# Sixteen dummy matmuls ahead of the first transposes in a fused attention and MLP kernel

## The chip, the cores and the metric

The kernel runs on one core of a Trainium2 chip. The metric is the device time of one execution in microseconds; lower is better. Times are medians of runs of the same state (all were undisturbed, "fast", or single runs, but for one run of the kernel with thirty-two dummies, which was classed slow and is left out of its ratio); positions "at 26.3 us" are counted from the start of the profiled execution.

## The reference

Eight batches of Nyström attention (8 heads, 576 positions, head size 64, 32 landmarks) followed by a two-layer MLP with a squared ReLU (512 to 2048 to 512) over 4608 tokens. Cut to what matters:

```python
q_lm = q.reshape(B, H, 32, 18, D).mean(axis=3)      # segment means, k alike
A, Bm, C = sm(q, k_lm), sm(q_lm, k_lm), sm(q_lm, k)  # three softmaxes
Z = Bm.T / (norm1(Bm) * norminf(Bm) + 1e-6)
for _ in range(6):
    Z = 2 * Z - Z @ Bm @ Z                           # iterative inverse
x = A @ Z @ C @ v                                    # then heads side by side
out = np.maximum(x @ w_in, 0) ** 2 @ w_out
```

## The kernel before

Each engine's order is written out by hand. `HEAD` is the order for batch 0, before any MLP work exists to fill PE (TensorE) with; later batches are woven into the MLP of the batch before them. Its first tokens, and what they do:

```python
HEAD = (
    "ck tk1 mk w:1:256 w:1:256 ek1d w:1:256 w:1 tk0 tt w:1 w:1 cq0 cq1 ek0a mq tq0 tq1 lm "
    ...
# ck      cast the loaded k to bf16, half on DVE, half on ACT
# tk, tq  PE transposes of k and q; ek, eq: their evacuation on DVE or ACT
# mk, mq  segment means on PE;  tt: transposes of the last positions
# cq      rearranging copy of q on DVE;  lm: landmark scores on PE
# w:n:c   n dummy matmuls of c columns (512 if not given)
```

The dummies write a PSUM bank that nobody reads until it is reused, and multiply a tile that DVE clears first:

```python
    bds = []
    for i in (1, 0):
        bd_t = const.tile([P, 2, NPAIR, P], BF16, name="bd%d" % i)
        nc.vector.memzero(bd_t[:])
        bds.insert(0, bd_t)
    ...
    def warm(n, width=512):
        z = bds[1].rearrange("p a b c -> p (a b c)")
        for _ in range(n):
            nc.tensor.matmul(idle[:, 0:width], lhsT=z[:, 0:P], rhs=z[:, 0:width],
                             start=True, stop=True)
```

POOL issues the loads of weights, v and the next batch, in this order, and then does a small copy and two memsets:

```python
LOADS = "w10 v0 w00 q1 w01 w11 o0 o1 o2 o3 v1"     # q1: k and q of batch 1
    ...
        with tc.issue_after(behind[0].ins):
            nc.gpsimd.tensor_copy(seg[:, NC4 + 2, :], seg[:, NC4, :])
            for i in range(2):
                ct = const.tile([P, 2, NC4 + 1, P], BF16, name="ct%d" % i)
                nc.gpsimd.memset(ct[:], 0.0)      # ct is read only from batch DMA_C = 9 on: never
                cts.append(ct)
```

DVE rearranges k and q of each further batch once they have landed (`stage` into `nat`), before PE transposes them:

```python
    def prepare(b: int, nm):
        ...
        nc.vector.tensor_copy(X[nm][:], raw)
```

The softmax here doesn't subtract the row's maximum and nothing guards it: scores larger than these inputs give would overflow.

Of the kernel before, what the change touches and what calls it, by code (L numbers as in the profile page):

```python
# [33 lines left out]
DMA_C = 9  # L34
COMPACT = 1
HEAD = (
    "ck tk1 mk w:1:256 w:1:256 ek1d w:1:256 w:1 tk0 tt w:1 w:1 cq0 cq1 ek0a mq tq0 tq1 lm "
    "w:1 et w:1:256 w:1 eq0a w:1:256 tl eq1d ls sum:0:4:5 w:1 ib w:1 w:1:256 sq1 w:1:256 if "
    "sk1 sum:1:2:5 w:1:256 w:1 sum:1:0:2 jo w:1:256 w:1:256 rec:1 w:1:256 row:1:0:3 "
    "row:1:3:5 w:1:256 sk0 w:1 sq0 jo w:1:256 w:1:256 w:1 w:1:256 sum:0:2:4 sum:0:0:2 w:1 jo "  # L40
    "rec:0 cv:0 cv:1 w:1:256 w:1:256 row:0:3:5 cr jo w:1:256 row:0:0:3 w:1:256 at:1 cba w:1 "
    "jl at:0 ea0d ea1a ct w:1:256 nu w:1:256 g:0 gl1d fv w:1 gf1d w:1 gf0a az gl0d"
# [933 lines left out]
```

## Time and profile before

| | before |
|---|---|
| time, median of 3 | 265.7 us (265.61 to 266.66) |
| profiled run | 266.55 us, span 264.8 us |
| first matmul | 8.01 us |
| PE busy | 94% of the span |
| first matmul of the MLP's second layer | 37.77 us |

How to read it: the page's slices give busy shares, but a PE that is busy at half speed looks as busy as one at full speed: 4.50 of 4.50 us from 8.5 to 13.0 us, with two 512-column dummies in 0.85 us, and 2.40 of 2.40 us from 47.3 to 49.7, with 225 ns for one 512-column matmul. The speed shows only where equal groups of matmuls are compared in the chain of waits (start, duration, what, how many) or in the timeline. The lines are in the prediction.

Some words of the texts stand for these spacings alone. PE is "cold", "asleep", its clock "down", where a 128-column transpose takes about 106 ns and a 512-column dummy 425 (before, 8 transposes and two dummies, 0.85 us each); it is "warm", "awake", its clock "up", where they take 55 to 56 and 215 ns. "Waking" and "release" are the change from the first to the second. That a clock is what changes is not shown: the granted clock of the page is full all through (mean 1.000). "Locked out" and "lockout" stand for q's copy taking 2.54 us in place of 0.68 beside POOL's work.

### The profile page before, as it was taken

The page shows a single profiled execution, that of the slowest core. Times are in us where ns is not written, and L with a number is a line of the kernel's source. Part 1 is how long each engine was busy: PE and PEld are TensorE (multiplying, and loading weights), DVE is VectorE, ACT ScalarE, POOL GpSimd, SP SyncE. Part 2 cuts the span into 40 slices and gives each one's busy share as a digit, 9 for nine tenths or more (in the row PEclk, how much of TensorE's full clock was granted, in tenths as well). Part 3 has the DMA queues.
Part 4 walks back from the last instruction along what each step waited for, and adds up shares of the span by engine and source line. Part 5 has one row for each costly group of instructions (what it writes and reads, how often), then busy time and mean ns, then how long its engine had stood idle before and what let it go on. Part 6 is the DMA issues. An engine that isn't in the chain of part 4 may idle for free.

```text
span 264.8 us, 6918 instructions
## 1 busy us (share of the span) xinstructions
PE 248.2 (94%) x2835; PEld 153.7 (58%) x2878; DVE 176.4 (67%) x485; ACT 158.5 (60%) x278; POOL 47.8 (18%) x73
## 2 busy tenths in 40 slices
PE   0799899999999999999999999999999999999994
PEld 0675665467665656566556565666566655555443
DVE  3488986879985779689766589689776884232100
ACT  1364887279666765678457565674777665365210
POOL 7744623302010500700003201320000000000000
PEclk9999999999999999999999999999999999999999
DMA  8999999998159899996829998999911111112122
GB/s 183 161 190 202 209 205 189 214 208 107 32 101 188 98 197 178 184 203 124 121 74 115 172 192 114 128 191 188 159 42 40 42 40 65 56 40 83 40 79 79
DMA packets 69791, 34.65 MB, mean 131 GB/s; under 512 B 37376, under 2 KB 64256, under 8 KB 69760
## 3 DMA queue, kind: packets, MB, share of 16 engines
q0 software_dynamic: 39808, 17.83, 54.2%
q1 hardware_dynamic: 24704, 7.08, 17.3%
q10 hardware_dynamic: 5248, 9.31, 11.3%
q8 instruction: 22, 0.36, 0.6%
q14 instruction: 9, 0.07, 0.1%
HBM read 36.70 MB, written 9.44 MB: 174 GB/s over the span
## 4 chain that ended last, share of the span: by engine, by line
PE 87%; DVE 5%; DMA 2%; issue 2%; ACT 2%; ACTq 0%
PE ops L853 24%; PE h L824 22%; PE n L853 21%; PE n L532 3%; PE g L807 3%; DMA stage<-in_k_dram 2%; PE idle L297 2%; PE n L416 2%; PE n L344 2%; PE n L598 2%; PE n L616 1%; DVE nat L283 1%; DVE gT L829 1%; PE tps L315 1%; PE n L631 1%
## 5 line engine op out<-in xcount | busy, mean ns | idle before, releaser
L828 ACT ACTIVATE r<-h 128x576 bf16<-128x576 f32 x128 | 81.3, 652 | 46.4 <-PE h L824 35.1
L853 PE MATMUL ops<-w_out_bf,gT 128*128 128x512 bf16 (+1 forms) x300 | 76.8, 368 | 0.9 <-issue 0.3
L853 PEld LDWEIGHTS <-gT 128*128 128x128 bf16 x592 | 53.2, 98 | 38.7 <-issue 4.2
L829 DVE TENSOR_TENSOR gT<-r 128x576 bf16<-128x576 bf16 x128 | 54.9, 448 | 26.3 <-ACT r L828 26.1
L824 PE MATMUL h<-AT,G 128*128 128x288 bf16 x448 | 71.0, 286 | 0.2
L853 PE MATMUL n<-w_out_bf,gT 128*128 128x512 bf16 x252 | 69.7, 379 | 1.1 <-issue 0.3
L824 PEld LDWEIGHTS <-G 128*128 128x128 bf16 x512 | 47.7, 97 | 24.3 <-issue 0.8
L705 DVE CAST G<-g 128x1024 bf16<-128x1024 f32 x14 | 17.1, 1224 | 5.4 <-PE g L807 5.4
L864 ACT COPY o_sb<-ops 128x512 f32<-128x512 f32 (+1 forms) x19 | 10.9, 574 | 14.5 <-PE ops L853 14.5
L864 ACT COPY o_sb<-n 128x512 f32<-128x512 f32 x17 | 10.0, 587 | 12.9 <-PE n L853 12.8
L705 ACT CAST G<-g 128x1024 bf16<-128x1024 f32 x14 | 14.2, 1013 | 4.5 <-PE g L807 4.5
L134 POOL DMA_DIRECT2D raw<-in_k_dram x5 | 4.6, 921 | 53.2 <-DVE gT L829 28.1
L532 PEld LDWEIGHTS <-T 128*128 128x128 bf16 x256 | 11.3, 98 | 4.2 <-issue 0.6
L574 DVE TENSOR_REDUCE ra<-EA 128x20 f32<-128x640 f32 (+3 forms) x19 | 13.2, 704 | 0.3 <-ACT EA L562 0.3
L586 DVE TENSOR_TENSOR an<-EA,rra 128x640 bf16<-128x640 f32 (+2 forms) x18 | 13.2, 736 | 0.2
L532 PE MATMUL n<-bd,T 128*128 128x64 bf16 x256 | 12.7, 193 | 0.3 <-issue 0.2
L315 PEld LDWEIGHTS <-nat 128*128 128x128 bf16 x96 | 6.8, 108 | 9.8 <-ACT nat L720 8.0
L537 ACT ACTIVATE EA<-n 128x512 f32<-128x512 f32 x16 | 9.6, 598 | 3.3 <-PE n L532 3.2
L134 POOL DMA_DIRECT2D raw<-in_q_dram x5 | 4.4, 884 | 38.5 <-DVE rc L447 28.1
L537 ACT ACTIVATE EC<-n 128x512 bf16<-128x512 f32 x16 | 9.5, 596 | 3.0 <-PE n L532 1.6
L315 PE MATMUL tps<-ident_bf,nat 128*128 128x128 bf16 x32 | 3.4, 278 | 8.0 <-ACT nat L720 8.0
L824 PE MATMUL h<-AZ,G 128*128 128x288 bf16 x64 | 10.0, 286 | 0.6 <-DVE AZ L797 0.4
(144 smaller groups left out, 294.6 us busy)
## 6 DMA issues: line engine op xcount, KB each, us to landing
out_dram<-o_sb ACTq DMA_DIRECT2D x31, 256.0 KB, 3.1
vm<-in_v_dram POOLq DMA_DIRECT2D x8, 512.0 KB, 10.1
raw<-in_k_dram POOLq DMA_DIRECT2D x5, 512.0 KB, 6.9
raw<-in_q_dram POOLq DMA_DIRECT2D x5, 512.0 KB, 6.1
w_in_bf<-in_moe_w_in_dram POOLq DMA_DIRECT2D x4, 512.0 KB, 12.1
w_out_bf<-in_moe_w_out_dram POOLq DMA_DIRECT2D x4, 512.0 KB, 17.2
out_dram<-o_sb ACTq DMA_DIRECT2D x9, 128.0 KB, 2.4
stage<-in_k_dram SPq DMA_DIRECT2D x1, 1024.0 KB, 6.1
```

The lines of the kernel that those rows point to most:

```text
L134: d = queue.dma_start(dst, src)
L315: nc.tensor.transpose(tps[:, i, p, :], X[nm][:, 2 * half + i, 2 * p:2 * p + 2, :].rearrange("p h d -> p (h d)"), ident_bf[:],)
L532: nc.tensor.matmul(sc[:, c, j, :, :], lhsT=X[nm + "T"][:, c, p, :], rhs=BD[:, 1 if nm == "q" else 0, p, 0:64], start=True, stop=True)
L537: nc.scalar.activation(dst, sc.rearrange("p c j i m -> p c (j i m)"), AF.Exp, scale=SCALE)
L574: nc.vector.reduce_sum(ra[:, quads, lo:hi, :], EA[:, quads, lo:hi, :].rearrange("p q c (h m) -> p q c h m", m=M), axis=AX.X)
L586: on.tensor_tensor(an[:, i, lo:hi, :].rearrange("p c (h m) -> p c h m", m=M), EA[:, i, lo:hi, :].rearrange("p c (h m) -> p c h m", m=M), r ...
L705: (act, dve)[n % 2](G[:, :, n * 512:n * 512 + 512], gg[:])
L824: nc.tensor.matmul(h[:, j, 0:HALF], lhsT=G[:, qd, f * P:(f + 1) * P], rhs=AT[:, qd, a0 + j * HALF:a0 + (j + 1) * HALF], start=(qd == 0), s ...
L828: nc.scalar.activation(r.rearrange("p (j t) -> p j t", j=2), h[:, :, 0:HALF], AF.Relu)
L829: return lambda: nc.vector.tensor_tensor(gT[:, f, o:o + S], r[:], r[:], ALU.mult)
L853: nc.tensor.matmul(ops, lhsT=gT[:, f, t * P:t * P + P], rhs=w_out_bf[:, f, i * n:i * n + n], start=(f == 0), stop=(f == NF - 1))
L864: nc.scalar.copy(o_h, ops)
```

## The change

The intent is to have PE busy while the first load is under way, so that it runs at full speed when real work arrives. The diff, whole (the other lines of `HEAD` are only broken anew):

```diff
 HEAD = (
-    "ck tk1 mk w:1:256 w:1:256 ek1d w:1:256 w:1 tk0 tt w:1 w:1 cq0 cq1 ek0a mq tq0 tq1 lm "
+    "w:16 ck tk1 mk w:1:256 w:1:256 ek1d w:1:256 w:1 tk0 tt w:1 w:1 cq0 cq1 ek0a mq tq0 tq1 "
```

## The prediction

Passages that rest on rules or figures which no trace or run of this case shows are cut out of the recorded texts, and the cuts are marked. In the prediction's sum this takes out the working of one term, the 0.1 us by which the dummies would hold the transposes on average. The sum came to 2.2 + 0.7 = 2.9 us of gain, less that 0.1: 2.8, and 266.55 - 2.8 = 263.75. What is left of the cost is its upper limit, all dummies cold, a hold of 0.37 us. Of rival 3 the share of held cases is cut, on which its lower figure, 0.2, rested, and of rival 1 the argument for and against. The 427 and 216 ns of a dummy are 425 ns (two in 0.85 us, before) and 215 ns in the traces; with 425 the 6.83 us would be 6.80.

> **What bounds the kernel now.** I read the page first: its busy shares, its slices, its chain.
>
> ```profile
> PE 248.2 (94%) x2835; PEld 153.7 (58%) x2878; DVE 176.4 (67%) x485; ACT 158.5 (60%) x278; POOL 47.8 (18%) x73
> ...
> PE   0799899999999999999999999999999999999994
> ...
> PEclk9999999999999999999999999999999999999999
> ...
> PE 87%; DVE 5%; DMA 2%; issue 2%; ACT 2%; ACTq 0%
> ```
>
> TensorE sets the end: 87% of the chain is PE. Only the first slice (6.6 us) is empty, while the first load of k comes in. The granted clock is full everywhere, so that row cannot show what this change is after; a slow PE start has to be read from how far apart equal matmuls begin. Next I took the chain in order of time from 7 to 15 us (start, us, what).
>
> ```profile
> 6.91 1.05 ACT nat L720
> 7.96 0.05 issue
> 8.01 1.03 PE tps L315 x8
> 9.04 0.53 PE n L344 x20
> 9.58 1.07 PE idle L297 x4
> 10.64 0.85 PE tps L315 x8
> 11.50 0.43 PE n L325 x4
> 11.92 0.85 PE idle L297 x2
> 12.78 0.53 PE n L344 x20
> 13.31 1.15 PE tps L315 x16
> ```
>
> From 8.01 to 14.46 us PE itself is the chain, with no wait in it. And it is slow: the second group of 8 transposes takes 0.85 us, 106 ns each, and two 512-column dummies 0.85 us, 425 ns each. The timeline of PE later shows the same shapes at half of that (start, duration, engine, line, operation).
>
> ```profile
> 28.14 0.61 PE L315 MATMUL n<-ident_bf,nat 128*128 128x128 bf16 x8
> 28.58 1.14 PE L824 MATMUL h<-AZ,G 128*128 128x288 bf16 x8
> ...
> 47.25 2.54 PE L853 MATMUL n<-w_out_bf,gT 128*128 128x512 bf16 x11
> 49.72 0.22 PE L416 MATMUL n<-y,U 32*32 32x32 bf16 x8
> ```
>
> Eight transposes advance from 28.14 to 28.58, 55 ns each; eleven 512-column matmuls from 47.25 to 49.72, 225 ns each. So PE starts at half speed. Where it changes: the 16 transposes that start at 13.15 are followed by the next kind at 14.29; with x at 106 and 16-x at 56 ns over 1.14 us, x is 5, so the change falls at about 13.7 us, 5.7 us after PE's first matmul.
>
> Last, the timelines of DVE and POOL about 27 us, because an earlier PE must meet the loads there.
>
> ```profile
> 27.47 0.42 DVE L666 COPY tT<-n 128x512 bf16<-128x512 bf16 x1
> 27.80 2.54 DVE L283 COPY nat<-stage 128x2048 bf16<-128x2048 bf16 x1
> ...
> 26.68 0.69 POOL L134 DMA_DIRECT2D vt<-in_v_dram  x1 [1.91 <-DMA stage<-in_q_dram]
> 27.36 0.22 POOL L261 COPY seg<-seg 128x32 bf16<-128x32 bf16 x1
> 27.50 2.28 POOL L264 MEMSET ct<- 128x1280 bf16 x2
> ```
>
> The rearranging copy of q of batch 1 takes 2.54 us; the same copy of k just before took 0.68. POOL's two memsets end at 29.78, and 29.78 plus the bulk of a normal copy is the copy's end at 30.34: it was locked out. POOL's wait that ends at 26.68 dates the landing of that q.
>
> [...]
>
> **The change part by part.** It removes and moves nothing; it puts 16 dummies of 512 columns at the head of PE's order, into a bank that nobody reads. They need only one cleared tile, the first of DVE's two memsets that run 0.99 to 2.01 us, so PE can start at about 1.55.
>
> Cost: cold, 16 x 0.427 = 6.83 us, ending at 8.38 at the latest, which would hold the transposes (now 8.01) by 0.37 us. [...]
>
> Saving up to the second group of transposes, cold from the chain, warm at half: k transposes 0.85 to 0.45, 0.40; dummies of 1280 columns 1.07 to 0.53, 0.54; k transposes 0.41; tail 0.43 to 0.22, 0.21; dummies of 1024 columns 0.42; the 16 q transposes 1.15 to 0.90, 0.25. The two groups of 20 segment means, 26 ns each already, save nothing. Sum 2.2 us.
>
> Can the other engines follow? Half q is copied by DVE at 10.55 to 11.36. With k's means 0.4 us earlier, DVE's two evacuations and that copy move up to end at about 10.8; PE gets to the q means at 10.6 and their first half needs only the first half of the copy. The evacuation of the second k group on ACT ends at about 11.1, when the last transposes need its bank. So PE is not held, and the landmark scores move from 14.29 to about 12.1. From there to 25 us PE, DVE and ACT alternate with no load in between (v landed at 16.7 and the first half of w_in at 20.4, as POOL's waits date them, needed at 18.1 and 21.2): all moves by 2.2.
>
> At the pair of copies: k of batch 1 landed at 23.9 and is copied at 26.21, so 24.0 just fits. The q copy would come at 25.6 but q lands at 26.65: 1.05 us is lost there. But it then starts with POOL's issue at 26.68, before POOL's memsets at 27.5, takes 0.68 and ends at 27.4 in place of 30.34: 2.9 earlier. PE reaches the q transposes at 29.72 - 2.2 = 27.5 (before it stood 0.66 us waiting for this copy), so the gain behind it is 2.2 + 0.7 = 2.9. [...] w_in's second half landed at 31.5 and w_out's first quarter at 34.0, needed at 34.9 - 2.9 = 32.0 and 37.8 - 2.9 = 34.9: still early enough. After 36 us PE is full and never waits longer than 0.2 us, so the gain lasts. Net 2.9 - 0.1 = 2.8 us.
>
> The profiled run took 266.55: 266.55 - 2.8 = 263.75. The timed runs are 265.61, 265.70 and 266.66. If the release moves [...], the two lower ones are runs with an early release, and the changed kernel, warm in any case, should reach about 263.7 from either. So against the median of 265.7 the gain is 2.0 us, 0.75%.
>
> **The rivals.** (1) Zeros or transposes don't wake PE, or the pause between the dummies' end [...] and 8.01 puts it to sleep again. [...] Then nothing is gained and up to 0.4 lost: 265.7 to 266.9. (2) The loads take it back: if the q copy loses its race with the memsets it ends at 30.3 as before and only a few tenths remain: about 265.5. Against: both start on the same landing, and POOL has 0.69 us of issuing and a copy first. (3) The dummies hold the transposes in every run because PE starts late (2.05, if both memsets are waited for): ends up to 8.9[...], gain smaller by 0.2 to 0.8: about 264.0 to 264.5. (4) DVE, on the chain for much of 25 to 36 us, keeps less than 0.7 of the copy's release: about 264.3.
>
> **Range and chances.** I predict 263.7 us, with 262.9 to 265.0 eight times in ten; the upper side holds rivals 3 and 4. Faster by over 2% would need 5.3 us, more than the whole cold stretch and the stall together can give: 0.02. Slower by over 2% has no path: 0.01. Within 2%: 0.97.
>
> **What would show it.** Dummies from about 1.6 us at 427 ns, later ones at 216; transposes at 8.0 to 8.4 at 56 ns each; landmark scores near 12.1; the q copy at 26.7 lasting 0.68; the matmuls of the first h after the q transposes near 28.6 in place of 31.49; later order and durations unchanged. Wrong if the first transposes still take 106 ns, if they start past 8.5, or if the copy is still above 2 us.

## The result

The changed kernel takes 263.85 us, median of 4 runs (263.62 to 264.05), against 266.0 for the kernel before (265.61 to 266.66, 4 runs). The ratio is 0.9917, 95% interval 0.9892 to 0.9941: within 2%, but clearly below one. Ratios are the mean time of one kernel's fast runs over that of the other's of the same rounds, so not quite the ratio of the medians.

The page of the changed kernel, busy shares and chain by engine:

```profile
PE 254.8 (97%) x2894; PEld 154.1 (59%) x2894; DVE 175.2 (67%) x485; ACT 158.3 (60%) x278; POOL 47.6 (18%) x73
...
PE 93%; DMA 2%; DVE 2%; ACT 1%; issue 0%
```

PE's share of the chain rose from 87 to 93%, and DVE's fell from 5 to 2%: a stretch that hung on DVE is gone. PE's timeline, from the start (start us, us, engine, line, operation, operands, how many, and in brackets what it waited for):

```profile
1.53 5.47 PE L297 MATMUL idle<-bd 128*128 128x512 bf16 x16 [1.53 <-DVE bd L117]
7.90 0.62 PE L315 MATMUL tps<-ident_bf,nat 128*128 128x128 bf16 x8 [0.91 <-ACT nat L720]
...
12.16 0.25 PE L374 MATMUL n<-STk,bd 128*128 128x32 bf16 x4
```

The dummies start with the first cleared tile and last 5.47 us; all cold they would take 6.8. With x of them at 0.425 us and the rest at 0.215 (two in 0.85 in before, two in 0.43 in its second profile), 5.47 less the 0.17 by which a last matmul outlasts its spacing (8 transposes at 28.14 in before: 0.61 us, the next kind 0.44 after their start) gives x = 8.9, so the estimate is that PE came to full speed at 5.3 us, inside the dummies. They end 0.9 us before the data. Here is the chain that followed, for comparison with the ten lines of before:

```profile
7.90 0.62 PE tps L315 x8
8.53 0.49 PE n L344 x20
9.02 0.55 PE idle L297 x4
9.57 0.45 PE tps L315 x8
10.02 0.22 PE n L325 x4
10.24 0.43 PE idle L297 x2
10.68 0.74 PE n L344 x20
11.42 0.90 PE tps L315 x16
```

Each wide group takes half of what it took: the second 8 transposes 0.45 us in place of 0.85, the dummies 0.55 in place of 1.07. Only the second group of means grew, 0.53 to 0.74: it waits for DVE's copy of q. The landmark scores moved from 14.29 to 12.16 us. Then DVE's timeline where q of batch 1 is copied, and POOL's beside it:

```profile
26.29 0.69 DVE L283 COPY nat<-stage 128x2048 bf16<-128x2048 bf16 x1 [0.53 <-DMA stage<-in_q_dram]
```

```profile
26.55 0.71 POOL L134 DMA_DIRECT2D vt<-in_v_dram  x1 [1.30 <-DMA stage<-in_q_dram]
27.25 0.22 POOL L261 COPY seg<-seg 128x32 bf16<-128x32 bf16 x1
27.39 2.28 POOL L264 MEMSET ct<- 128x1280 bf16 x2
```

DVE now waits for q (0.53 us), starts the copy on its landing, ahead of POOL, and is done at 26.98 in place of 30.34. (POOL waits for the same landing and issues 0.26 us after DVE's start, so POOL's issue of v dates the landing a little late.) PE's transposes of k of batch 1 (x8) and of q behind them (x16), in the changed kernel:

```profile
26.01 0.61 PE L315 MATMUL n<-ident_bf,nat 128*128 128x128 bf16 x8
...
27.43 1.06 PE L315 MATMUL n<-ident_bf,nat 128*128 128x128 bf16 x16
```

and those of q in the kernel before, where those of k start at 28.14 (a line of the prediction):

```profile
30.39 1.07 PE L315 MATMUL n<-ident_bf,nat 128*128 128x128 bf16 x16 [0.66 <-DVE nat L283]
```

PE no longer waits for the copy. The third pair of h starts at 28.37 in place of 31.49, the MLP's second layer at 34.64 in place of 37.77. That is 3.1 us; the profiled runs differ by 2.9 (266.55 and 263.62).

### The profile page after: what moved, and what is told of

Read it like the earlier page. It is cut to its first block, busy times and chain, and to the rows that moved or that the text cites. A ratio compares the mean times of both kernels' runs of the same rounds, so it can differ in the third digit from the quotient of the medians.

```text
span 261.9 us, 6993 instructions
## 1 busy us (share of the span) xinstructions
PE 254.8 (97%) x2894; PEld 154.1 (59%) x2894; DVE 175.2 (67%) x485; ACT 158.3 (60%) x278; POOL 47.6 (18%) x73
## 4 chain that ended last, share of the span: by engine, by line
PE 93%; DMA 2%; DVE 2%; ACT 1%; issue 0%
PE ops L853 25%; PE h L824 24%; PE n L853 23%; PE g L807 3%; PE n L532 3%; PE n L344 2%; DMA stage<-in_k_dram 2%; PE idle L297 2%; PE n L416 2%; PE n L598 2%; PE n L616 1%; PE n L315 1%; PE n L631 1%; PE tps L315 1%; PE n L560 1%; ACT r L828 1%
## 5 line engine op out<-in xcount | busy, mean ns | idle before, releaser
L853 PE MATMUL ops<-w_out_bf,gT 128*128 128x512 bf16 (+1 forms) x320 | 81.7, 368 | 0.0
L853 PE MATMUL n<-w_out_bf,gT 128*128 128x512 bf16 x272 | 74.5, 379 | 0.0
L297 PE MATMUL idle<-bd 128*128 128x512 bf16 (+1 forms) x51 | 13.5, 379 | 1.5 <-DVE bd L117 1.5
L416 PEld LDWEIGHTS <-ED 128*128 128x128 bf16 x72 | 6.8, 98 | 6.2 <-DVE EY L455 0.6
```

Source lines behind the costliest of these rows:

```text
L416: nc.tensor.matmul(res[a:a + w, qd, :], lhsT=diagonal[a:a + w, qd, :], rhs=moving(qd)[a:a + w], start=True, stop=True)
L853: nc.tensor.matmul(ops, lhsT=gT[:, f, t * P:t * P + P], rhs=w_out_bf[:, f, i * n:i * n + n], start=(f == 0), stop=(f == NF - 1))
```

## The experiments

One relation holds through all runs and makes them easy to read: the time of a profiled run less the start of the first second-layer matmul is 228.8 to 229.1 us in all thirteen profiles that were taken. So the whole scatter and the whole gain are made in the first 38 us; the rest is a PE that is full. A second relation divides these 38 us. From PE's first transposes of k of batch 1 to that first second-layer matmul it takes 8.63 or 8.64 us in all seven profiles in which q's copy was neither stalled nor held back, and in none of them does PE wait for the copy. It takes 9.52 to 9.97 us in the five profiles with a stalled copy, and 11.30 us in the one with a copy held on purpose. So the start of the k transposes shows what the head cost, and the excess over 8.63 us what the copy cost.

| kernel (profiled run) | first transposes | landmark scores | q copy, us | k transposes of batch 1 | second layer starts | time of that run | that run's PE at full speed from |
|---|---|---|---|---|---|---|---|
| before | 8.01 | 14.29 | 27.80, 2.54 | 28.14 | 37.77 | 266.55 | 13.7 |
| before again, a | 7.66 | 12.84 | 26.34, 2.87 | 26.68 | 36.65 | 265.73 | 10.7 |
| before again, b | 7.69 | 13.26 | 26.77, 2.42 | 27.11 | 36.63 | 265.62 | 11.6 |
| changed | 7.90 | 12.16 | 26.29, 0.69 | 26.01 | 34.64 | 263.62 | 5.3 |

### Narrow dummies

```diff
-    "w:16 ck
+    "w:16:32 ck
```

> The same 16 dummies at the head, but 32 columns wide instead of 512: the same place in PE's order, the same wait for the cleared tile, too short to make PE busy (under 1 us). Theory (the dummies earn only by waking PE's clock): PE is cold again at its first transposes, 104 to 106 ns each, and the time is that of the kernel before, ratio 0.997 to 1.003. Rival (what helps is that PE has already passed its first wait and fetched its program, whatever the width): 2 us faster, ratio 0.992.

Measured: ratio 0.9995 (0.9958 to 1.0032), 265.25 us against 265.7. PE's timeline:

```profile
1.53 0.61 PE L297 MATMUL idle<-bd 128*128 128x32 bf16 x16 [1.53 <-DVE bd L117]
7.69 1.03 PE L315 MATMUL tps<-ident_bf,nat 128*128 128x128 bf16 x8 [5.55 <-ACT nat L720]
```

Sixteen instructions in the same place, but 0.61 us of work: the first eight transposes take 1.03 us as before, not 0.62. It was the length of the work that counted here, not its place in the order.

### Eight dummies

```diff
-    "w:16 ck
+    "w:8 ck
```

> 8 dummies of 512 columns, 3.4 us cold, ending at about 4.9 us: [...] then a pause of 3 us up to the first transposes. Theory [...]: nearly never woken, PE cold at 7.9 us, ratio 0.996 to 1.002. Rival ([...] a pause of 3 us doesn't matter): as fast as with 16, ratio 0.991 to 0.993.

Measured: ratio 0.9999 (0.996 to 1.0039), but spread from 263.76 to 266.62 us: one of the six runs as fast as the changed kernel, the others not. The chain of the profiled run (264.49 us):

```profile
7.67 0.62 PE tps L315 x8
8.29 0.49 PE n L344 x20
8.79 0.98 PE idle L297 x4
9.77 0.85 PE tps L315 x8
...
12.42 0.90 PE tps L315 x16
```

The dummies ran from 1.53 to 5.13 us, all slow (8 x 0.425 is 3.40, and a cold matmul outlasts its spacing by 0.2: 8 transposes at 10.44 in before took 1.06 us, the next kind came 0.85 after their start). Yet the first transposes are at full speed (8 in 0.62 us, 1.03 when cold), and the next group, 2 us later, is at half speed again (0.85 us); the third is fast (16 in 0.90). So PE came to full speed at the end of the dummies or after it, was slow again about 1.2 us after the pause that ended at 7.67 (estimated from the 0.98 us of the four older dummies, 1.07 cold and 0.55 warm), and came up once more. The theory's time was right in the mean; the reason it gave was not shown, and what it expected of PE ("nearly never woken") was wrong in this run. That the pause of 2.5 us slowed PE again is the reading of this one profile, not shown apart from other causes; it speaks against the rival. If so, sixteen dummies fill the pause as well as wake PE.

### The kernel before without POOL's memsets

```diff
-                nc.gpsimd.memset(ct[:], 0.0)
```

> The kernel before without POOL's two memsets of a tile that this configuration never reads; no dummies at the head. Theory (0.7 us of the gain came from q's copy getting ahead of the memsets): the copy takes 0.68 us in place of 2.54 and the time falls by 0.4 to 0.8 us, ratio 0.997 to 0.9985; the cold start stays. Rival (the copy's lockout was hidden elsewhere): ratio 0.999 to 1.001. Second rival (the lockout is the larger part of the gain): ratio under 0.995.

Measured: ratio 0.9968 (0.9941 to 0.9995), 264.74 us (264.15 to 264.97); the copy took 0.68 us, the first transposes were cold as before (8 in 1.04 us). A little more than expected: about 0.85 us of the gain can be had without waking PE ahead of its first work. POOL's small copy stayed in; in the profiled run it shared only 0.05 us with q's copy (26.98 to 27.20, and 27.15 to 27.83). The spread also shrank from 2.2 us to 0.8.

### The changed kernel without the memsets

The same line is taken out.

> The changed kernel without those memsets. Theory (it already runs the copy ahead of them): no further gain, ratio to the kernel before 0.991 to 0.993, the same as the changed kernel, copy 0.68 us. Rival (the memsets still hold some DVE instruction in the changed kernel): another 0.3 to 0.7 us, ratio 0.989 to 0.990.

Measured: ratio 0.9928 (0.9902 to 0.9955), 263.6 us (263.34 to 263.9). No further gain, as the theory had it. Between this kernel and the last one only the 16 dummies differ, both are free of the memsets, and both ran on the same chip: 264.74 to 263.6, 1.1 us for PE's speed. The profiled runs show where: k transposes at 27.49 and 26.20 us, and 8.63 us more to the second layer in both.

### The kernel before without its older dummies

```diff
-    "ck tk1 mk w:1:256 w:1:256 ek1d w:1:256 w:1 tk0 tt w:1 w:1 cq0 ...
+    "ck tk1 mk ek1d tk0 tt cq0 ...
```

> The kernel before with the six older dummies (2304 columns, 1.9 us cold on the chain) ahead of q's segment means taken out and nothing put in. Rival to the change (these dummies are the cost: dropping them pays as much as waking PE ahead): transposes and means move up, up to 1.9 us faster, ratio 0.993 to 0.995. Theory ([...] q's copy on DVE holds PE anyway): the stretch stays cold past 14 us and the time is between 0.7 us faster and 1.5 us slower, ratio 0.997 to 1.006.

Measured: ratio 0.9939 (0.9899 to 0.9979), 264.05 us, in two clumps: 263.47, 263.64, 263.69 and 264.4 on the one side, 265.38 and 265.78 on the other. That is the rival's number. The profiled run was one of the upper clump; its 16 q transposes took 1.71 us in the chain, 107 ns each, so PE was still at half speed at 13.1 us, as the theory said, and its copy of q took 2.55 us. Both were half right. No profile shows a run of the fast clump; that such runs escape the stall of q's copy is argued here, not shown; the clean kernel below only shows what this head takes when the stall cannot happen.

### Thirty-two dummies

```diff
-    "w:16 ck
+    "w:32 ck
```

> 32 dummies in place of 16. The first 9 cold and the rest at 216 ns end at about 10.4 us if PE is woken at 5.3 us[...]; the first transposes wait for them, 2.5 to 4 us late. Theory (the gain is the warm stretch minus any hold of the transposes): the saving of 2.2 is more than spent and q's copy falls among the memsets again: 266 to 268 us, ratio 1.000 to 1.009. Rival (the later wait for the loads of batch 1 swallows a late start): within 0.3 us of the changed kernel, ratio 0.991 to 0.993.

Measured: 265.34, 266.6 and 268.79 us, and 270.35 us in a run that was slow and doesn't count; ratio 1.0041 (0.9982 to 1.01), in the theory's range. In the profiled run, the fastest, the dummies held the first transposes until 9.79 us; but the copy of q did not fall among the memsets, as the theory had it: it started close to its landing (27.40, 0.68 us). What was lost there is PE's lateness: k transposes at 27.74, 1.73 us after the changed kernel's, and 1.72 us more time. The one profile doesn't show why the two other fast runs lost 1.3 and 3.5 us more, and that stays open.

### The kernel before, profiled twice more

No edit.

> The kernel before, unchanged, for another profile. Theory (the moment at which PE is woken moves [...] and that is the kernel's own scatter of 1 us): the release, read from the transposes' spacing, is at another moment than 13.7 us, and the time follows it at about half a microsecond per microsecond. Rival (scatter comes from the loads): the release is at 13.7 again, whatever the time.

> The kernel before once more, for a third profile: the same expectation as for the run before it, release and time together.

Measured: 265.73 and 265.62 us. PE came to full speed at 10.7 us in the first (four of the second eight transposes are slow: 0.65 us in all) and at 11.6 in the second, so the moment does move; what moves it is not shown. But the time did not follow: the landmark scores were 0.42 us apart, 12.84 and 13.26, and the second layer started at 36.65 and 36.63. What made them meet again is in DVE's timeline and POOL's of the first of them:

```profile
26.34 2.87 DVE L283 COPY nat<-stage 128x2048 bf16<-128x2048 bf16 x1
29.13 1.69 DVE L829 TENSOR_TENSOR gT<-r 128x576 bf16<-128x576 bf16 x4
```

```profile
26.17 0.69 POOL L134 DMA_DIRECT2D vt<-in_v_dram  x1 [1.82 <-DMA stage<-in_q_dram]
26.86 2.41 POOL L261 COPY seg<-seg 128x32 bf16<-128x32 bf16 x1
29.21 2.26 POOL L264 MEMSET ct<- 128x1280 bf16 x2
```

Here it was not the memsets. DVE's copy and POOL's small copy, which takes 0.22 us elsewhere, overlapped, and both lasted until 29.2 us. In the other run DVE's copy began at 26.77 and POOL's at 26.84, with the same end, 29.19. The end is tied to POOL's start, that is to the landing of q (POOL issues v on the same landing, 26.17 and 26.16), and not to how early DVE was ready. The profile of before in the prediction had q land half a microsecond later and met the memsets instead. So in these three profiles the end is set by the landing and the collision; the moment of the release sets only when PE and DVE arrive there.

### The changed kernel with q's copy held back

```diff
-        nc.vector.tensor_copy(X[nm][:], raw)
+        moved = nc.vector.tensor_copy(X[nm][:], raw)
+        if (b, nm) == (1, "q"):
+            tc.add_manual_dep(moved.ins, held[0].ins.name, ...)   # the second memset
```

> The changed kernel with q's copy of batch 1 made to wait for POOL's second memset: the clock is awake from the start, but the copy ends about 30.3 us as in the profile of before. Theory (a held copy absorbs whatever PE gained ahead of it): nothing of the gain is left, ratio 0.998 to 1.002, third pair of h near 31.4 us. Rival (the warm stretch carries its 2 us past the copy, the collision is a small extra): ratio 0.992 to 0.996.

Measured: ratio 1.0048 (0.9994 to 1.0101), 267.24 us (266.12 to 268.08). DVE's timeline and PE's:

```profile
29.74 0.69 DVE L283 COPY nat<-stage 128x2048 bf16<-128x2048 bf16 x1 [3.39 <-POOL ct L264]
```

```profile
30.49 1.07 PE L320 MATMUL n<-ident_bf,nat 128*128 128x128 bf16 x16 [2.32 <-DVE nat L283]
```

The landmark scores were at 12.35 us, as early as in the changed kernel. DVE waited 3.39 us, PE 2.32, the third pair of h started at 31.59 and nothing was left; the loss against before beyond the expected range fits a copy ending at 30.4, later than in the two typical runs of before (29.2). A warm start was worth nothing here, with this copy ending late.

### No dummies, no collision

The older dummies and the memsets are taken out as above, and POOL's small copy moves to where POOL is idle:

```diff
         band(seg[:, s, :], [[SEG, M]], SEG - 1 - t0, -1)
+    nc.gpsimd.tensor_copy(seg[:, NC4 + 2, :], seg[:, NC4, :])
```

> No dummies at the head at all: the kernel before without the six older dummies ahead of q's means, without POOL's two memsets, and with POOL's small copy moved to its idle time near 6 us, so that nothing can collide with q's copy. Theory (with the collision gone the cold start is still worth about 1 us): 264.0 to 264.8 us, ratio 0.993 to 0.996. Rival (the collision is all that mattered, the clock nothing): the time of the changed kernel, ratio 0.991 to 0.9925.

Measured: ratio 0.9926 (0.9901 to 0.9952), 263.95 us (263.81 to 264.37): just between the two ranges. The chain, DVE's timeline and PE's (line numbers are one lower in this kernel):

```profile
11.43 1.71 PE tps L314 x16
```

```profile
26.48 0.68 DVE L282 COPY nat<-stage 128x2048 bf16<-128x2048 bf16 x1
```

```profile
26.82 0.61 PE L314 MATMUL n<-ident_bf,nat 128*128 128x128 bf16 x8
```

By the medians, nearly all of the gain is there. But the profiled run, in which PE is cold to 13.1 us, was the slowest of the six (264.37 us). Its k transposes start 0.81 us after the changed kernel's, nothing stalls behind them, and its time is 0.75 us longer than that kernel's profiled run: there this cold head still costs about 0.8 us, near the theory's 1 us. Whether PE woke earlier in the faster runs no profile shows. With the older dummies gone, PE waits on DVE for much of the stretch (the second means start at 10.59, held by the copy of batch 0's q), and DVE reaches the copy of batch 1's q at 26.48, 0.11 us after POOL's issue of v.

### A try at something better

```diff
-    "w:16 ck tk1 mk w:1:256 w:1:256 ek1d w:1:256 w:1 tk0 tt w:1 w:1 cq0 cq1 ek0a mq ...
+    "w:16 ck tk1 mk cq0 cq1 ek1d tk0 tt ek0a mq ...
```

together with the edits to POOL of the run before.

> A try at something better: the 16 dummies, without the six older ones, q's copy of batch 0 ahead of the evacuation of the first k transposes on DVE, POOL cleaned as in the run before. Theory (PE reaches q's copy of batch 1 a few tenths earlier, but that copy waits for its load in any case): 263.2 to 263.8 us, ratio 0.990 to 0.993, landmark scores at 11.4 to 11.9 us. Rival (the head is still the bound): another 0.7 us or more, ratio under 0.990.

Measured: ratio 0.9912 (0.9889 to 0.9935), 263.66 us, with the smallest spread of all (263.52 to 263.77). The landmark scores came at 11.79 us, but the copy of k of batch 1 began beside POOL's issue of v and took 1.11 us in place of 0.69. That copy is on the chain (1.02 us of it), and k transposes start at 26.16 us, no earlier than in the changed kernel (26.01). Q's copy ends at 26.62, well before PE needs it at 27.58. So it was at the copy of k, and not, as the theory had it, at the landing of q, that the earlier head was lost. The kernel is not clearly faster than the changed one (0.9917 on its own rounds).

## Why the prediction was right, and where it was not

The time (263.7 predicted, 263.85 measured) and most of the way there held. Step by step:

- **Start and end of the dummies.** Predicted 1.55 us and an end at 8.38 at the latest; they ran from 1.53 to 7.00 and did not hold the transposes. Rival 3 fell with that. (The mean hold of 0.1 us in the sum was the author's estimate from figures that no run shows. No hold was seen.)
- **Saving on PE.** Predicted 2.2 us up to the landmark scores; the profiles show 14.29 to 12.16, 2.1, of which 0.1 is an earlier load of k. Group by group the two chains give 2.25 us of savings, less the 0.21 by which the q means got longer because they now wait for DVE. The prediction had PE not held there; that was too hopeful by those 0.2 us.
- **The race at q's copy.** Predicted to start with the landing at 26.7 and to end at 27.4; it started at 26.29 and ended at 26.98. Predicted gain behind it 2.2 + 0.7 = 2.9, seen 28.14 - 26.01 = 2.1 from an earlier PE and 9.63 - 8.63 = 1.0 from the copy, 3.1 in all. The second term was too small: it counted only PE's own wait of 0.66 us. Rivals 2 and 4 fell.
- **No later loss.** The 228.8 to 229.1 us from the first second-layer matmul to the end are the same in every profile.
- **Rival 1.** Zeros alone did wake PE: the 16 dummies took 5.47 us in place of 6.8, so their own spacing changed (at 5.3 us, by the estimate above), before any other matmul. After the pause of 0.9 us the first transposes were at full speed (8 in 0.62 us); with eight dummies and a pause of 2.5 us PE fell back to half speed about 1.2 us after the pause (one profile). So this rival named a danger that did not show with sixteen dummies.

The step that failed is the reading of the scatter: that the two lower times of before "are runs with an early release". The release does move, 10.7 to 13.7 us in three profiles, and the two early ones do go with the lower times. But two runs with releases 0.9 us apart ended within 0.1 us of each other, because a collision between DVE's and POOL's copies, timed by the landing of q, made them wait for the same moment. Against these two the change brought 0.7 and 1.1 us from an earlier PE and 1.3 and 0.9 us from the copy. So the gain of 2.0 us against the median came out, but an early release alone was not the reason; that it fitted so well is partly luck.

The two parts also depend on each other. While the end of the copy is fixed by POOL, an earlier PE only waits longer: with the copy held back, an awake PE gained nothing (1.0048). With the memsets gone the parts can be had one by one: a cold PE gained 0.85 us (0.9968), and an awake one another 1.1 (0.9928). And once the six older dummies and POOL's small copy are out of the way as well, a kernel without dummies at the head comes within 0.3 us of the best one with them (263.95 against 263.66 of the same rounds, in the last two runs). So the change buys two things: PE reaches batch 1 earlier (0.7 to 2.1 us, against the three profiles of before), and DVE is ready for q's copy before POOL gets to its own work (0.9 to 1.3 us). Among the profiles with the memsets in the program, the held one aside, the copy stalled for 1.7 us or more in all five in which it began over 0.15 us after POOL's issue of v (before, its two repeats, the narrow dummies, the kernel without older dummies), and in none of the three in which it began ahead of that issue or within 0.1 us of it (changed, eight, thirty-two). The prediction named the memsets as the thing to collide with; in four of those five it was POOL's small copy ahead of them.

What stays open: why two short overlapping copies both take 2.4 us or more, why 32 dummies lost up to 3.5 us more in other fast runs, and whether POOL's small copy alone, without memsets behind it, would stall q's copy (the one profile that has it so shows only 0.05 us of overlap, and no stall).

## What to carry to other kernels

Read PE's speed from the spacing of equal matmuls in the trace, not from its busy share: here a PE that ran its first eight transposes in 1.03 us ran them in 0.62 after 5.47 us of matmuls on zeros while the first load was under way. Look at the pause that they leave before real work (here 0.9 us did no harm; with one of 2.5 us, in one profile, PE was slow again 1.2 us later). Then follow the lead that this gives to the next thing that doesn't move with it, here a load and a neighbour engine's work timed by the same load: the lead can vanish there, or, if it wins a race, grow. Before adding work to win a race, look whether the other party (here memsets of a tile that nobody reads) is needed at all.

## What else the profiles show

- In the changed kernel without memsets PE woke after some 2.8 us of dummies (16 of them in 4.98 us; worked out as above, 6.5 slow ones), in the changed kernel after 3.8 us (1.53 to 5.3); both are estimates. With eight dummies it was slow again at about 8.9 us although it had worked since 7.67 us (the first 0.6 us of that on transposes). Sixteen matmuls of 512 columns on zeros were followed by fast first transposes (8 in 0.62 us) in all four profiles that had them (changed, without the memsets, with the copy held, the last try).
- Transposes showed both speeds too: 56 ns each once PE was awake (8 in 0.45 us) and 106 ns before (8 in 0.85 us).
- In four profiles (two of before, the narrow dummies, the kernel without older dummies) DVE's copy started 0.07 to 0.52 us ahead of a POOL copy, and it still took 2.42 to 2.87 us in place of 0.68 while the POOL copy took 2.41 in place of 0.22. (POOL's spans are rough in these profiles, but DVE's next instruction, at 29.0 to 29.2 us, confirms the end.) Beside the memsets, in the first profile of before, it took 2.54 us. Beside POOL's issuing of a load, which began first each time, now one and now the other was lengthened: the issue took 1.06 us in place of 0.69 when q's copy began 0.11 us after it (the kernel without dummies and collision), and the copy of k took 1.11 us in place of 0.69 when it began 0.27 us after it (the last kernel).
